# Two of 64 stores issued as two DMAs each in a group-normalisation kernel

## The chip, the cores and the metric

The kernel runs on one core of one Trainium2 chip. The metric is the device time of one execution in microseconds (us), as the median over runs; lower is better.

## The reference

Group normalisation over 128 samples of 1024 channels by 32 x 16 pixels, in 32 groups of 32 channels, all in bfloat16:

```python
def reference(x, g, b):
    G = 32
    B, C, H, W = x.shape[0], x.shape[1], x.shape[2], x.shape[3]
    xr = x.reshape(B, G, C // G, H, W)
    mu = xr.mean(axis=(2, 3, 4), keepdims=True)
    var = ((xr - mu) ** 2).mean(axis=(2, 3, 4), keepdims=True)
    xn = (xr - mu) / jnp.sqrt(var + 1e-5)
    xn = xn.reshape(B, C, H, W)
    return xn * g[None, :, None, None] + b[None, :, None, None]
```

`x` is normal noise times 0.05, `g` is close to 1 and `b` close to 0. Input and output are 134 MB each.

## The kernel before

The work is cut into 64 tiles. A tile `xt` holds two samples: 128 partitions (rows), and in each row 16 channels of 512 pixels, 8192 values or 16 KB. A group of 32 channels lies in two neighbouring rows. A tile is one contiguous piece of 2 MB in the input and in the output, and a row is a contiguous 16 KB of it.

Each tile passes through these steps, one function each:

- `L(i)` loads the tile with one DMA (L121).
- `M1(i)` (L137, ACT) sums the last quarter of each row; `M(i)` (L154, TensorE) sums the rest with an indicator matrix that also adds the two rows of a group. Tiles 0 and 1 are summed by TensorE alone. `R(i)` (L171, DVE) turns the sums into the negative mean.
- `Q(i)` (L189, ACT) squares the centred values and sums them; `Gm(i)` (L206, TensorE) adds the rows of a group; `T(i)` (L221, ACT) takes the square root.
- `A(i)` (L232 to L255, DVE) forms scale and bias for each channel and applies them in place, in 16 instructions, one for each channel of a row.
- `S(i)` stores the tile with one DMA (L267).

The steps of different tiles are interleaved by hand: the main loop's round `s` issues `M1` and `M` of tile `s+1`, `Gm` of `s-1`, `A` of `s-2`, `R` of `s+1`, `Q` of `s`, `T` of `s-1`, then `S` of `s-2` and `L` of `s+7`. A helper, `chain`, ties each instruction to the one before it on the same engine, so every engine runs in the order in which the program is written.

All transfers are issued by one queue, SP's, in that order: nine loads ahead of the loop (and after the first of them four small loads of `g` and `b`), then store, load, store, load. There are eleven `xt` buffers. So `L(i+9)`, which stands behind `S(i)`, goes into the buffer of tile `i-2` and waits until `S(i-2)` has landed, and `S(i+1)` waits in the same queue behind it. After the last load the last nine stores stand in a row, each waiting only for its tile's `A`.

The completion of a transfer is told by a semaphore. There are eight of them, taken in turn, and a transfer that takes one waits, where nothing else ensures it, until the transfer eight places before it has landed. Completion is counted by 16, one for each DMA engine.

The function that the change touches is `S`:

Of the kernel before, what the change touches and what calls it, by code (L numbers as in the profile page):

```python
# [18 lines left out]
PREFETCH = 9  # L19
MM_FREE = 512  # L20
ACT_CHUNKS = 4


@with_exitstack
def kernel(
# [7 lines left out]
    nc = tc.nc  # L33
    P = nc.NUM_PARTITIONS
# [18 lines left out]
    NMM = F // MMN  # L53
    assert 0 <= ACT_CHUNKS < NMM

    x_v = x.rearrange("(t n) (cb k) h w -> t (n cb) (k h w)", n=NS, cb=CB)
    o_v = out.rearrange("(t n) (cb k) h w -> t (n cb) (k h w)", n=NS, cb=CB)
# [19 lines left out]
    def chain(key, inst):  # L77
        prev = last.get(key)
        if prev is not None:
            tc.add_manual_dep(inst.ins, prev.ins.name, nosync, reason="pipeline order")  # L80
        last[key] = inst
        return inst
# [5 lines left out]
        out=ind_f[:].rearrange("p (a c) -> p a c", c=PPG),  # L88
        in_=ones_f[:].rearrange("p (a c) -> p a c", c=PPG),
# [7 lines left out]
        out=ind_f[:].rearrange("p (a c) -> p a c", c=PPG),  # L97
        in_=ind_f[:].rearrange("p (a c) -> p a c", c=PPG),
# [25 lines left out]
    def act_part(i):  # L124
        return ACT_CHUNKS if i >= 2 else 0

# [137 lines left out]

    def S(i):
        st = state[i]
        chain("sp", nc.sync.dma_start(out=o_v[i], in_=st["xt"][:]))  # L267
        state.pop(i - 3, None)

    for i in range(min(PREFETCH, NT)):  # L270
# [16 lines left out]
    for s in range(-1, NT + 2):  # L287
        if 0 <= s + 1 < NT:
            M1(s + 1)
            M(s + 1)  # L290
        if 0 <= s - 1 < NT:
            Gm(s - 1)
        if 0 <= s - 2 < NT:
            A(s - 2)
        if 0 <= s + 1 < NT:
            R(s + 1)
        if 0 <= s < NT:
            Q(s)
        if 0 <= s - 1 < NT:
            T(s - 1)  # L300
        if 0 <= s - 2 < NT:
            S(s - 2)
            if s - 2 + PREFETCH < NT:
                L(s - 2 + PREFETCH)
# [30 lines left out]
```

## Time and profile before

| | |
|---|---|
| median of 3 runs | 639.6 us (639.49 to 640.18) |
| span of the profiled execution, first to last instruction | 637.8 us |
| between that span and the median of the runs | 1.8 us |
| moved by DMA | 268.69 MB, mean 421 GB/s over the span |
| time of ACT's pieces for one tile: L189, L137 | 7.12 and 1.90 us (means) |
| store, median from issue to landing | 28.7 us |
| load, median from issue to landing | 24.2 us |
| issue and landing of the last store | 621.0 us, 15.7 us later |

The profile comes from one execution, its times count from the first instruction. Its page gives the busy time of each engine, the busy share in 40 equal slices of the span, the DMA queues, the chain of work that ended last, and the costliest groups of instructions. The trace behind it also answers for single stretches of time: which instructions ran, what ended the wait before them, and what share of the 16 DMA engines was moving packets. A share of 1.00 means all 16 at work, 0.06 is one of them.

### The profile page before, as it was taken

How to read it: one execution, taken by the hardware profiler on the slowest of the kernel's cores; microseconds unless marked ns; L12 is line 12 of the kernel's file. 1: busy time of each engine (PE TensorE's matmuls, PEld its weight loads, DVE VectorE, ACT ScalarE, POOL GpSimd, SP SyncE). 2: the span in 40 equal slices, each digit the busy share in tenths (PEclk: the TensorE clock that was granted, in tenths of full speed). 3: DMA queues.
4: the chain of work that ended last, by engine and by line, in shares of the span. 5: the costliest groups of instructions: out<-in, count | busy, mean ns of one | idle time of the engine just before them, and what ended most of it. 6: DMA issues, size and time to landing. Idle time of an engine off the chain costs nothing.

```text
span 637.8 us, 3899 instructions
## 1 busy us (share of the span) xinstructions
PE 326.3 (51%) x887; PEld 127.1 (20%) x904; DVE 421.0 (66%) x1349; ACT 590.7 (93%) x318; POOL 1.6 (0%) x6
## 2 busy tenths in 40 slices
PE   4654564556456555645654664464553654635300
PEld 1221122122112212211221222121221221212100
DVE  0086677668667766866776686677667667767680
ACT  1999999999999999999999999999999999999920
POOL 1000000000000000000000000000000000000000
PEclk9767767776776676666667667766766667666655
DMA  8999999999999999999999999999999999999993
GB/s 357 427 427 426 428 425 429 434 428 423 434 429 429 430 431 432 430 431 430 432 429 431 432 431 431 428 431 433 431 429 430 432 432 430 429 432 431 430 423 163
DMA packets 18774, 268.69 MB, mean 421 GB/s; under 512 B 2368, under 2 KB 2368, under 8 KB 2368
## 3 DMA queue, kind: packets, MB, share of 16 engines
q1 hardware_dynamic: 18752, 268.45, 98.7%
q8 instruction: 7, 0.11, 0.1%
q14 instruction: 15, 0.12, 0.0%
HBM read 134.23 MB, written 134.22 MB: 421 GB/s over the span
## 4 chain that ended last, share of the span: by engine, by line
ACT 53%; DMA 23%; issue 17%; DVE 2%; PE 1%; SPq 0%; DVEq 0%; ACTq 0%
ACT ja L189 38%; DMA out_dram<-xt 18%; ACT ja L137 14%; DMA xt<-in_x_dram 5%; DVE xt L255 2%; ACT rstd L221 1%; PE ps L154 1%; SPq L121 0%; DVE jd L171 0%; DVE bia L243 0%; DVE scl L237 0%; DVEq L330 0%; DVE rstd L232 0%; ACTq L137 0%
## 5 line engine op out<-in xcount | busy, mean ns | idle before, releaser
L189 ACT ACTIVATE ja<-xt,negmean 128x8192 bf16<-128x8192 bf16 x64 | 455.8, 7122 | 15.2 <-DVE jd L171 13.2
L154 PE MATMUL ps<-xt,ind_b 128*128 128x512 bf16 x759 | 301.9, 576 | 80.3 <-DMA xt<-in_x_dram 73.1
L255 DVE TENSOR_SCALAR xt<-xt,scl,bia 128x512 bf16<-128x512 bf16 x1024 | 336.6, 408 | 2.6 <-DVE bia L243 0.2
L154 PEld LDWEIGHTS <-ind_b 128*128 128x128 bf16 x776 | 108.6, 146 | 244.8 <-issue 162.4
L232 DVE RECIPROCAL rstd<-rstd 128x1 f32<-128x1 f32 x64 | 10.5, 164 | 169.1 <-ACT rstd L221 169.1
L137 ACT ACTIVATE ja<-xt 128x2048 bf16<-128x2048 bf16 x62 | 117.7, 1898 | 2.6 <-DMA xt<-in_x_dram 2.6
L243 DVE SCALAR_TENSOR_TENSOR bia<-scl,negmean,bet 128x16 f32<-128x16 f32 x64 | 15.0, 235 | 2.3
L237 DVE TENSOR_SCALAR scl<-gam,rstd 128x16 f32<-128x16 f32 x64 | 15.0, 234 | 2.2
L189 ACT ACTIVATION_READ_ACCUMULATOR ja<-xt,negmean 128x1 f32 x64 | 11.9, 186 | 0.0
L137 ACT ACTIVATION_READ_ACCUMULATOR ja<-xt 128x1 f32 x62 | 11.7, 189 | 0.0
L171 DVE TENSOR_SCALAR_CACHE_REDUCE jd<-ps 128x512 bf16<-128x512 f32 x2 | 1.4, 692 | 7.9 <-PE ps L154 7.9
L171 DVE TENSOR_SCALAR_CACHE_REDUCE jd<-ps,ps_170 128x512 bf16<-128x512 f32 x1 | 0.8, 755 | 6.6 <-PE ps_170 L206 6.6
L284 DVE CAST gam<-gam_b 128x16 f32<-128x16 bf16 x1 | 0.2, 174 | 6.4 <-DMA gam_b<-in_g_dram 6.4
L206 PE MATMUL ps_3186<-carry,ind_f 128*128 128x1 f32 x2 | 0.6, 362 | 6.7 <-ACT ja L189 6.7
L206 PE MATMUL ps_2155<-carry,ind_f 128*128 128x2 f32 x2 | 0.6, 362 | 4.8 <-ACT ja L137 4.8
L206 PE MATMUL ps_930<-carry,ind_f 128*128 128x2 f32 x2 | 0.6, 364 | 4.8 <-ACT ja L137 4.8
L206 PE MATMUL ps_1812<-carry,ind_f 128*128 128x2 f32 x2 | 0.6, 364 | 4.7 <-ACT ja L137 4.7
L206 PE MATMUL ps_587<-carry,ind_f 128*128 128x2 f32 x2 | 0.6, 364 | 4.7 <-ACT ja L137 4.7
L206 PE MATMUL ps_1469<-carry,ind_f 128*128 128x2 f32 x2 | 0.6, 362 | 4.6 <-ACT ja L137 4.6
L206 PE MATMUL ps_244<-carry,ind_f 128*128 128x2 f32 x2 | 0.6, 364 | 4.6 <-ACT ja L137 4.6
L206 PE MATMUL ps_1126<-carry,ind_f 128*128 128x2 f32 x2 | 0.6, 364 | 4.6 <-ACT ja L137 4.6
L206 PE MATMUL ps_2008<-carry,ind_f 128*128 128x2 f32 x2 | 0.6, 362 | 4.6 <-ACT ja L137 4.6
(319 smaller groups left out, 126.9 us busy)
## 6 DMA issues: line engine op xcount, KB each, us to landing
xt<-in_x_dram SPq DMA_DIRECT2D x64, 2048.0 KB, 24.2
out_dram<-xt SPq DMA_DIRECT2D x64, 2048.0 KB, 28.7
gam_b<-in_g_dram SPq DMA_DIRECT2D x2, 2.0 KB, 7.1
bet_b<-in_b_dram SPq DMA_DIRECT2D x2, 2.0 KB, 6.7
```

What stands on the lines that cost most here:

```text
L137: nc.scalar.activation(out=ja[:, 0 : na * MMN], in_=xt[:, (NMM - na) * MMN :], func=ACT.Identity, scale=-inv_n, accum_out=carry[:, 1:2],),
L154: nc.tensor.matmul(out=ps[:], lhsT=ind_b[:], rhs=xt[:, k * MMN : (k + 1) * MMN], start=(k == 0), stop=(k == npe - 1),),
L171: nc.vector.tensor_scalar(out=jd[:], in0=st["ps"][:], scalar1=-inv_n, scalar2=seed, op0=ALU.mult, op1=ALU.add, accum_out=negmean[:],),
L189: nc.scalar.activation(out=ja[:], in_=st["xt"][:], func=ACT.Square, bias=st["negmean"][:], scale=1.0, accum_out=carry[:, 0:1],),
L206: nc.tensor.matmul(out=ps2[:, 0:ncol], lhsT=ind_f[:], rhs=st["carry"][:, 0:ncol], start=True, stop=True,),
L221: nc.scalar.activation(out=rstd[:], in_=st["ps2"][:, 0:1], func=ACT.Sqrt, bias=eps_t[:], scale=inv_n),
L232: chain("dve", nc.vector.reciprocal(out=rstd[:], in_=rstd[:]))
L237: nc.vector.tensor_scalar(out=scl[:], in0=gam[:], scalar1=rstd[:], scalar2=None, op0=ALU.mult),
L243: nc.vector.scalar_tensor_tensor(out=bia[:], in0=scl[:], scalar=negmean[:], in1=bet[:], op0=ALU.mult, op1=ALU.add,),
L255: nc.vector.tensor_scalar(out=xt[:, k * HW : (k + 1) * HW], in0=xt[:, k * HW : (k + 1) * HW], scalar1=scl[:, k : k + 1], scalar2=bia[:, k ...
L284: nc.vector.tensor_copy(out=gam[:], in_=gam_b[:])
```

## The change

A table names two tiles and a row for each. The stores of these two tiles are issued as two DMAs, one right behind the other on SP's queue: rows 0 to 119 and 120 to 127 for tile 20, rows 0 to 87 and 88 to 127 for tile 40. The other 62 stores, all loads and all compute are written as before.

```diff
@@ -19,6 +19,7 @@
 PREFETCH = 9
 MM_FREE = 512
 ACT_CHUNKS = 4
+STORE_CUTS = {20: 120, 40: 88}
 
 
 @with_exitstack
@@ -264,7 +265,12 @@
 
     def S(i):
         st = state[i]
-        chain("sp", nc.sync.dma_start(out=o_v[i], in_=st["xt"][:]))
+        cut = STORE_CUTS.get(i)
+        if cut is None:
+            chain("sp", nc.sync.dma_start(out=o_v[i], in_=st["xt"][:]))
+        else:
+            chain("sp", nc.sync.dma_start(out=o_v[i][0:cut], in_=st["xt"][0:cut, :]))
+            chain("sp", nc.sync.dma_start(out=o_v[i][cut:P], in_=st["xt"][cut:P, :]))
         state.pop(i - 3, None)
 
     for i in range(min(PREFETCH, NT)):
```

In the program that results, SP issues 134 DMAs instead of 132, and the two more take a place each in the turn of the eight semaphores. The second pieces and the stores of the next three tiles after each cut carry a wait for the transfer eight places before. The instructions of the other engines are the same, in the same order; only their line numbers move by one and by six.

## The prediction

> **What bounds the kernel now.** I read the page first: its busy table, the DMA rows of the 40 slices and the queue list.
>
> ```profile
> span 637.8 us, 3899 instructions
> PE 326.3 (51%) x887; PEld 127.1 (20%) x904; DVE 421.0 (66%) x1349; ACT 590.7 (93%) x318; POOL 1.6 (0%) x6
> DMA  8999999999999999999999999999999999999993
> DMA packets 18774, 268.69 MB, mean 421 GB/s; under 512 B 2368, under 2 KB 2368, under 8 KB 2368
> q1 hardware_dynamic: 18752, 268.45, 98.7%
> ```
>
> ACT (93%) and the 16 DMA engines (98.7%) are nearly level. To see which ends last, I listed ACT's tile starts (L137) near the end.
>
> ```profile
> 524.21 1.90 ACT L137 ACTIVATE ja<-xt 128x2048 bf16<-128x2048 bf16 x1
> 533.50 1.90 ACT L137 ACTIVATE ja<-xt 128x2048 bf16<-128x2048 bf16 x1
> ...
> 582.72 1.91 ACT L137 ACTIVATE ja<-xt 128x2048 bf16<-128x2048 bf16 x1 [0.32 <-DMA xt<-in_x_dram]
> 592.43 1.91 ACT L137 ACTIVATE ja<-xt 128x2048 bf16<-128x2048 bf16 x1 [0.31 <-DMA xt<-in_x_dram]
> ```
>
> Up to 533.5 us ACT runs at its own pace, 9.29 us a tile; for the last six tiles it waits for loads, at 9.71 us a tile. A tile is one load and one store, 256 rows of 16 KB, 16 rows on each of 16 DMA engines: **9.71 / 16 = 0.607 us for a row on one engine**. Then the windows of the tail, whose last two columns are the DMA engines' mean share and GB/s:
>
> ```profile
> 600.00:620.00 20.00, 1.17 (x4) 1.00 (x4) 16.57 (x55) 9.34 (x7) 0.00 (x0) 0.52 1.01 431
> 626.00:627.00 1.00, 0.00 (x0) 0.00 (x0) 0.00 (x0) 0.00 (x0) 0.00 (x0) 0.50 0.88 377
> 627.00:628.00 1.00, 0.00 (x0) 0.00 (x0) 0.00 (x0) 0.00 (x0) 0.00 (x0) 0.50 0.38 164
> 629.00:630.00 1.00, 0.00 (x0) 0.00 (x0) 0.00 (x0) 0.00 (x0) 0.00 (x0) 0.50 0.15 66
> 633.00:634.00 1.00, 0.00 (x0) 0.00 (x0) 0.00 (x0) 0.00 (x0) 0.00 (x0) 0.50 0.08 33
> 635.00:636.00 1.00, 0.00 (x0) 0.00 (x0) 0.00 (x0) 0.00 (x0) 0.00 (x0) 0.50 0.08 33
> ```
>
> All 16 engines are busy to 620 us, six at 627.5 (0.38 x 16), two at 629.5, and from 631 to 636 only **one**. The list of DMA packets from 630 us confirms it: a row at a time, in even steps.
>
> ```profile
> DMA  0400020020002002000200200020020002000000
> ```
>
> The trace also holds the 16 completions of each transfer, one from each engine. Those of the last store come at 627.1 us for the first, then, the latest five, 628.4, 628.9, 629.7, 631.3 and 636.7. The spread was 0.5 us in the first loads, 5.2 us near 230 us, 8.4 us near 430 us and 10.6 us for the second-last store. So one engine falls behind all the way, and a transfer is complete only when that engine is. The last load, too, was whole only at 592.3, when its fastest engine had been done for 10.1 us. Most of its loss comes in nine steps of about 0.9 us from 158 to 598 us, each 1 to 6 us after one of the queue-14 instruction packets. I call it the straggler. It sets the end: 636.7, 1.1 us before the span closes.
>
> **The change, part by part.**
>
> *The bytes.* Nothing is added or removed: both pieces together hold the same 128 rows. What can move is which engine carries them. A whole transfer gives each engine eight rows. For 120, 8, 88 and 40 rows the trace has no example. I bound it from both sides: dealt as evenly as whole rows allow, no engine gains or loses over about two rows, 1.2 us; dealt in the eight-row shares that every transfer of this trace has, 120 rows fill 15 engines and leave one without, 88 fill 11 and leave five without; the 8 rows make one row each on eight engines, the 40 four each on ten. I take the second, because 120 and 88 are whole multiples of the one share the trace shows, and I take the engines as filled from one end of their order. Against 16 rows for the two stores, the first eight engines then carry 8+1 and 8+4 rows, 21, five more: 5 x 0.607 = **+3.0 us**. The next two carry 20: +2.4 us. One carries 16: 0. Four carry 8: 8 x 0.607 = -4.9 us. The last carries none: **-9.7 us**.
>
> [...]
>
> *The end.* All engines have work queued until the last store, so a shift of rows at tiles 20 and 40 is carried to the end whole. With the straggler the one that carries none, it would finish at 636.7 - 9.7 = 627.0 and another becomes last: 631.3, 629.7 and 628.9 are the next, each +3.0 if it is among the first eight, so 634.3, 632.7 or 631.9. I take the middle one, with the 631.3 engine among those relieved: 636.7 - 632.7 = **4.0 us saved**. The bounds are 2.4 us (634.3) and 5.3 us (628.4 + 3.0).
>
> *Does compute let it?* The last store is issued at 621.0. The shifted engines finish the store before it at 621.3 + 3.7 + 3.0 = 628.0 in the middle case, so they don't wait for the last issue. ACT follows earlier loads: without load waits its last tile could start at 533.50 + 6 x 9.29 = 589.2 rather than 592.4. The loads' latest engine is up to 4 us earlier after the change.
>
> *Two more issues on SP.* Each costs 0.33 to 0.45 us of its queue (the store's issue time, L267). Behind each stands one load, and behind that the next store. They are hidden by the queued work: a load lands a median 24.2 us after its issue, five transfers of 4.86. Price 0; uncovered, 2 x 0.45 = 0.9 us.
>
> *New waits.* The program reuses eight completion semaphores in turn, so the second piece, and the stores of the next three tiles, wait for the transfer eight places earlier, before an unbroken line of loads and stores. For the second piece of tile 20 that is the load of tile 25. The load issued just before had already waited for the store of tile 17, which stands behind tile 25 in every engine's line. The same holds for the others: price 0. The loads that reuse the two buffers wait for both pieces; at most one or four rows on an engine, within the sum.
>
> The sum: 0 + 0 - 4.0. The profiled execution is 637.8 long, 1.8 below the 639.6 median, so 637.8 - 4.0 = 633.8 there and **635.6 us** in the runs.
>
> **Where the straggler sits** no row tells: the trace doesn't number the engines. The same engine is delayed at every step, so the instruction packets come on a fixed one; a fixed duty is more likely given to an end of the order than to its middle, and of the two ends I favour the one that the pieces reach last. That is a choice. [...]
>
> **Rivals.**
> - *The straggler gets more rows* (slower). If it is among the first eight, its end moves to 636.7 + 3.0: 639.6 + 3.0 = 642.6; at place nine or ten 642.0. For it: ten of 16 places. It decides as soon as the straggler's extra exceeds zero, since nothing else ends within 5.4 us. Against it: the argument of the ends.
> - *Two engines read the same part of SBUF.* If in whole transfers each engine always has the same eight rows, engines that are dealt other rows may meet in one part of the memory. If that doubles an eight-row share, each cut store costs 4.9 us more on the loaded engines: 635.6 + 9.7 = 645.3; at half the clash 640.5. For it: the rate of 26.9 GB/s an engine (431 / 16) is nearly steady through the run, as if each had a lane to itself. Against it: by tile 20 the completions are spread over 3.9 us without the straggler, six rows, which thins out a clash. [...]
> - *The pieces are dealt evenly*, so the change moves no work: 639.6 (straggler ±1.2 at most), or the straggler is the place with 16 rows: 639.6. For it: 16 completions of every transfer here; against it: half rows would be needed for 120 and 88.
> - *The straggler loses only eight rows* (among the four): it ends at 631.9, and 632.7 still stands: also 635.6.
>
> **How the numbers follow.** Straggler without rows 0.46, straggler with eight fewer 0.12: together 0.58 for 635.6, with a range of its own from 634.0 (just below 639.6 - 5.3) to 637.2 (639.6 - 2.4). Even or unmoved: 0.10. Straggler with more rows: 0.23. Clash on reads: 0.09. About 0.2% (1.3 us) is what can be told from no change here. So faster 0.58, same 0.10, slower 0.32. The whole range runs from 633.8 to 643.0, over the straggler's 642.6; only a full clash lies outside.
>
> **What would show it.** Right: one engine's late run from 631 to 636 is gone, the DMA share falls from 1 to 0 within a shorter tail, some engines end their last store early, and the last load lands before 592. The short pieces would have fewer completions that follow data. Wrong on dealing: tail unchanged. Wrong on place: the lone engine works 3 us longer. Clash: packets of the two cut stores, near 235 and 425 us, take more than their usual 0.61 us, and the DMA row of those slices falls.

## The result and the profile after

The changed kernel takes 643.87 us (median; 642.93 to 644.09) against 639.55 us of the kernel before on the same chip: 4.3 us more, a ratio of 1.0063 with a 95% interval of 1.005 to 1.0075. It is slower, where the prediction had 635.6 us, and just above its range.

First the rate in 40 slices of 16 us in the kernel before, 423 to 434 GB/s but for the first and the last slice:

```profile
GB/s 357 427 427 426 428 425 429 434 428 423 434 429 429 430 431 432 430 431 430 432 429 431 432 431 431 428 431 433 431 429 430 432 432 430 429 432 431 430 423 163
```

and the span, the rate and the queue of the changed kernel:

```profile
span 642.4 us, 3909 instructions
GB/s 358 429 422 424 429 427 430 431 429 428 432 431 432 428 431 385 431 432 428 434 428 433 431 426 436 429 433 410 392 433 427 432 431 429 433 426 434 429 376 199
q1 hardware_dynamic: 18764, 268.45, 98.6%
```

The bytes are the same. The rate dips at two places, in the 16th slice and in the 28th and 29th, where the cut stores are moved, and in the 39th, before the end. The windows around the two places (the last two columns are the DMA engines' mean share and GB/s), before:

```profile
244.00:256.00 12.00, 5.39 (x14) 2.06 (x14) 7.42 (x25) 11.97 (x9) 0.00 (x0) 0.72 1.00 429
442.00:458.00 16.00, 9.58 (x26) 3.53 (x27) 12.00 (x38) 15.94 (x8) 0.00 (x0) 0.68 1.01 432
```

and after:

```profile
244.00:256.00 12.00, 5.53 (x14) 2.06 (x14) 7.14 (x24) 11.97 (x9) 0.00 (x0) 0.72 0.99 369
442.00:458.00 16.00, 6.07 (x16) 2.24 (x16) 12.31 (x39) 15.94 (x8) 0.00 (x0) 0.68 1.01 379
```

The engines are as busy as before (0.99 and 1.01) and move 12 to 14% less: packets there take longer than their 0.61 us, 0.69 us on average from 242 to 256 us and 0.70 us from 442 to 458 us. No engine stands idle, the rows themselves are slow. Then the windows of the tail, after:

```profile
600.00:620.00 20.00, 3.53 (x13) 2.03 (x11) 15.65 (x52) 14.63 (x7) 0.00 (x0) 0.59 0.94 401
632.00:633.00 1.00, 0.00 (x0) 0.00 (x0) 0.00 (x0) 0.00 (x0) 0.00 (x0) 0.50 0.46 197
634.00:635.00 1.00, 0.00 (x0) 0.00 (x0) 0.00 (x0) 0.00 (x0) 0.00 (x0) 0.50 0.34 147
636.00:637.00 1.00, 0.00 (x0) 0.00 (x0) 0.00 (x0) 0.00 (x0) 0.00 (x0) 0.50 0.27 115
638.00:639.00 1.00, 0.00 (x0) 0.00 (x0) 0.00 (x0) 0.00 (x0) 0.00 (x0) 0.50 0.19 82
640.00:641.00 1.00, 0.00 (x0) 0.00 (x0) 0.00 (x0) 0.00 (x0) 0.00 (x0) 0.50 0.08 33
```

Before, all engines were busy to 620 us. Now the share is already 0.94: engines that are ahead run out of work, since the last stores are issued late, the last one at 626.3 us (621.0 before). And the late ones are later: five engines at 634.5 (0.34 x 16), four at 636.5, three at 638.5, one or two at 640.5. The last completions of the last store, singly, are 637.1, 637.5, 640.1, 641.0 and 641.4 us, where they had been 628.4, 628.9, 629.7, 631.3 and 636.7. The last load is late too: ACT starts its last tile at 597.7 us in place of 592.4.

In this profiled execution the engine that ends last is not the straggler. The straggler can be told by its steps of 0.8 to 1 us behind instruction packets. Those behind the packets at 485.0, 543.6 and 601.6 us appear in the third-latest or second-latest completion, not in the latest. So the straggler ends at 640.98 us, 4.2 us later than its 636.75 before, and another engine ends 0.4 us behind it. That other engine ended at 631.4 us or sooner before the change. Five more rows explain 3.0 of its 10 us; about 7 us have another cause.

The completions also tell how the rows were dealt. With a full transfer 16 data completions come. The 120-row piece has 15, the 8-row piece 8, the 88-row piece 11 and the 40-row piece 10. (Each of these has one completion more, half a microsecond after its issue, before any of its data.)

### The profile page after: what moved, and what is told of

Its sections match the earlier page's. It is cut to its first block, busy times and chain, and to the rows that moved or that the text cites. A ratio compares the mean times of both kernels' runs of the same rounds, so it can differ in the third digit from the quotient of the medians.

```text
span 642.4 us, 3909 instructions
## 1 busy us (share of the span) xinstructions
PE 328.3 (51%) x887; PEld 128.5 (20%) x904; DVE 420.8 (66%) x1349; ACT 591.7 (92%) x318; POOL 1.6 (0%) x6
## 4 chain that ended last, share of the span: by engine, by line
ACT 49%; DMA 27%; issue 15%; DVE 5%; PE 1%; DVEq 0%; SPq 0%; ACTq 0%
ACT ja L190 36%; DMA out_dram<-xt 14%; DMA xt<-in_x_dram 13%; ACT ja L138 13%; DVE xt L256 4%; ACT rstd L222 1%; PE ps L155 1%; DVE jd L172 0%; DVE bia L244 0%; DVE scl L238 0%; DVE rstd L233 0%; DVEq L336 0%; SPq L122 0%; ACTq L138 0%
## 5 line engine op out<-in xcount | busy, mean ns | idle before, releaser
L155 PE MATMUL ps<-xt,ind_b 128*128 128x512 bf16 x759 | 305.1, 581 | 89.5 <-DMA xt<-in_x_dram 86.4
L207 PE MATMUL ps<-carry,ind_f 128*128 128x2 f32 (+1 forms) x128 | 31.7, 318 | 197.0 <-ACT ja L138 185.5
L207 PEld LDWEIGHTS ps<-carry,ind_f 128*128 128x128 f32 x128 | 30.0, 278 | 230.7 <-ACT ja L138 211.2
L172 DVE TENSOR_SCALAR_CACHE_REDUCE jd<-ps,ps 128x512 bf16<-128x512 f32 x62 | 46.3, 746 | 7.1 <-PE ps L207 7.1
L222 ACT ACTIVATE rstd<-ps,eps_t 128x1 f32<-128x1 f32 x64 | 15.4, 241 | 0.5 <-PE ps L207 0.5
L172 DVE DVE_READ_ACCUMULATOR jd<-ps,ps 128x1 f32 x62 | 4.9, 80 | 0.0
```

Of the source, the lines that this page charges most:

```text
L155: nc.tensor.matmul(out=ps[:], lhsT=ind_b[:], rhs=xt[:, k * MMN : (k + 1) * MMN], start=(k == 0), stop=(k == npe - 1),),
L172: nc.vector.tensor_scalar(out=jd[:], in0=st["ps"][:], scalar1=-inv_n, scalar2=seed, op0=ALU.mult, op1=ALU.add, accum_out=negmean[:],),
L207: nc.tensor.matmul(out=ps2[:, 0:ncol], lhsT=ind_f[:], rhs=st["carry"][:, 0:ncol], start=True, stop=True,),
L222: nc.scalar.activation(out=rstd[:], in_=st["ps2"][:, 0:1], func=ACT.Sqrt, bias=eps_t[:], scale=inv_n),
```

## The experiments

Two theories stand against each other. PLACE: the straggler is not among the engines relieved, but among the first eight, which carry five rows more. CLASH: the place does not matter; engines that are dealt other rows than usual slow each other. In all runs the kernel before ran beside the others on the same chip; differences are between medians.

### One cut at a time

The first of the two runs cuts tile 20 alone,

```diff
-STORE_CUTS = {20: 120, 40: 88}
+STORE_CUTS = {20: 120}
```

and the second tile 40 alone:

```diff
-STORE_CUTS = {20: 120, 40: 88}
+STORE_CUTS = {40: 88}
```

> Only tile 20's store is cut, 120 + 8 rows. Theory PLACE (the straggler is one of the first eight engines, so the cut adds rows to the very engine that ends last; nothing else costs): one row more, 0.61 us, 639.55 + 0.6 = 640.2 us. Theory CLASH (the cost is that engines that are dealt other rows than usual disturb each other: in the changed kernel's packets from 242 to 256 us the time above 0.61 us sums to 26 us over 15 engines, 1.7 us each, on average): 641.3 us or more. If both act on the straggler: 641.9.

> Only tile 40's store is cut, 88 + 40 rows. PLACE: the straggler carries 12 rows in place of 8, four more, 2.4 us: 642.0. CLASH alone (from 442 to 458 us the time above 0.61 us sums to 32 us over 11 engines, 2.9 us each): 642.4. Both on the straggler: 644.8. The two cuts are expected to add up to the 4.3 us of the changed kernel.

Measured: 641.24 against 639.78 (ratio 1.0023, 1.0014 to 1.0031), 1.5 us; and 643.02 against 639.78 (1.0046, 1.0034 to 1.0058), 3.2 us. They add up to 4.7 us, which agrees, within the intervals, with the 4.3 of both. Each lies above PLACE, by 0.9 and 0.8 us; the first is clear of noise, while the interval of the second (2.2 to 3.7 us) still holds PLACE's 2.4. So either PLACE and a smaller second cost, or CLASH at about its own price; the next two runs separate these.

### A clash without extra rows, and extra rows without a clash

```diff
-STORE_CUTS = {20: 120, 40: 88}
+STORE_CUTS = {20: 64, 40: 64}
```

> Tiles 20 and 40 are cut in the middle, 64 + 64 rows. If rows are dealt in equal shares to as many engines as divide the count, all 16 engines get four rows of each piece, eight in all, as before, so PLACE expects no change, 639.6. CLASH expects engines to meet in the rows of one half: packets of these two stores well above 0.61 us, the rate of those slices down from 431 GB/s to 340 or less, and 641 to 645 us.

The other run leaves the stores whole and puts eight extra copies between two tensors in device memory behind stores:

```diff
+EXTRA = {12: (8, 1), 16: (8, 1), 20: (8, 1), 24: (8, 1), 28: (8, 1), 32: (8, 1), 36: (8, 1), 40: (8, 1)}
...
+    scr = nc.dram_tensor("scr", (ncopy, rcopy, F + 2048), BF16, kind="Internal").ap()
...
+        rows, times = EXTRA.get(i, (0, 0))
+        for _ in range(times):
+            chain("sp", nc.sync.dma_start(out=scr[nscr[0]][0:rows, 0:F], in_=x_v[i][0:rows]))
+            nscr[0] += 1
```

A pair in the table is the number of rows and of copies.

> No store is cut; eight extra copies of 8 rows of 16 KB from the input to a scratch tensor in device memory, one behind the store of tiles 12, 16, ... 40: one row more on each of the first eight engines each time, and no SBUF in it. PLACE: the straggler carries 8 x 0.607 = 4.9 us more: 644.4 us. If the straggler is one of the other eight engines, as the prediction took it, the end stays where it was unless the second slowest engine (5.4 us ahead) is overtaken: 639.6. CLASH has no part in it.

The halves: 641.65 against 639.78 (1.0034, 1.0019 to 1.005), 1.9 us, 0.9 a cut, with 16 completions for each half and so eight rows a store on every engine. Single runs of this kernel lie further apart than those of the kernel before, from 640.4 to 645.2 us. Its windows at the same two places:

```profile
244.00:256.00 12.00, 5.55 (x14) 2.06 (x14) 7.20 (x24) 11.97 (x9) 0.00 (x0) 0.72 1.00 370
442.00:458.00 16.00, 7.18 (x19) 2.66 (x20) 12.23 (x39) 15.94 (x8) 0.00 (x0) 0.68 1.00 392
```

Nearly the same dip, 370 and 392 GB/s at full share, though not down to the 340 expected. So the dip, which is CLASH's sign, comes without any imbalance.

The extra copies: 644.59 against 639.78 (1.0072, 1.006 to 1.0084), 4.8 us for eight rows, 0.60 a row. PLACE had 4.9, and the prediction's placing of the straggler had 0. The tail of this run:

```profile
632.00:633.00 1.00, 0.00 (x0) 0.00 (x0) 0.00 (x0) 0.00 (x0) 0.00 (x0) 0.50 0.16 66
638.00:639.00 1.00, 0.00 (x0) 0.00 (x0) 0.00 (x0) 0.00 (x0) 0.00 (x0) 0.50 0.08 33
640.00:641.00 1.00, 0.00 (x0) 0.00 (x0) 0.00 (x0) 0.00 (x0) 0.00 (x0) 0.50 0.04 16
```

The lone engine is there as before (a share of 0.06 on average), but works until 641 where it stopped at 636. The straggler took the extra rows: PLACE is shown, and CLASH is a second cost beside it.

### Which engine it is

In the changed kernel the 8-row piece had 8 data completions, one row on each of eight engines. The same extra copies with fewer rows are taken to reach fewer engines in the same way, from the same end. Only the number of rows in the table differs.

> As the run with eight extra copies, but of 7 rows each, so that the eighth engine gets none. If the straggler is one of the first seven: again 4.8 us more, 644.6. If it is the eighth: its end stays, 639.7, unless the second slowest, 5.4 us ahead before, overtakes it with 8 x 0.607 = 4.9 us: at most 640. [...]

> Eight extra copies of 4 rows, so one row more on the first four engines each time. If the straggler is one of these: 639.9 + 4.8 = 644.7. If it is the fifth, sixth or seventh: 640, or a little more if the second slowest overtakes.

> Eight extra copies of 2 rows, one row more on each of the first two engines. If the straggler is one of these: 644.7; if not: 640.

> Eight extra copies of 3 rows, one row more on each of the first three engines. Two rows left the end where it was and four moved it by 4.6 us, so the straggler is the third or the fourth engine: 644.5 if the third, 640 if the fourth.

| rows in each of 8 extra copies | this, us | before, us | ratio (95%) |
|---|---|---|---|
| 8 | 644.59 | 639.78 | 1.0072 (1.006 to 1.0084) |
| 7 | 644.94 | 640.15 | 1.0074 (1.0062 to 1.0086) |
| 4 | 644.48 | 639.85 | 1.007 (1.0056 to 1.0085) |
| 3 | 639.89 | 639.78 | 1.0003 (0.9993 to 1.0012) |
| 2 | 639.88 | 639.85 | 0.9999 (0.999 to 1.0008) |

Three rows cost nothing (639.89 us), four cost the whole 4.6 us (644.48). So the straggler is the fourth engine in the order in which these copies are dealt, number 3 counted from 0. In the trace of the four-row run the latest completion also rises by 0.6 us behind copies, between its larger steps; in that of the three-row run it does not. The runs were made on four chips, two and four rows on one of them and three rows on another, so the place is taken to be the same on each; all five rows of the table agree with that.

The runs with two and three rows carry eight more DMAs than the kernel before, with their issues, semaphores and waits, at no cost (639.88 and 639.89 us), which also clears those parts of the change.

### What the clash is

> Six stores (tiles 8, 16, 24, 32, 40, 48) cut into 64 + 64 rows; every engine keeps eight rows a store. If what is left over beside the extra rows is the clash of engines that are dealt rows other than their own, it grows with the cuts: 0.9 us a cut by the run with two such cuts, 639.9 + 6 x 0.9 = 645.3. If the two-cut run was a stray: 640.

> The same six stores cut by columns, 128 rows of 8 KB each, twice. Each engine keeps its own rows; there are as many DMAs, semaphores and waits as with the cut by rows, and twice the packets. CLASH: no engine meets another, so no change: 639.9, packets of half the size at half the time, and the rate stays at 431 GB/s. If it is the second DMA itself that costs (its issue, its semaphore, its wait), the same 5 us as the cut by rows.

The second of these cuts the same six stores by columns:

```diff
-        chain("sp", nc.sync.dma_start(out=o_v[i], in_=st["xt"][:]))
+        cols = [0, F // 2, F] if i in COLUMN_CUTS else [0, F]
+        for lo, hi in zip(cols, cols[1:]):
+            chain("sp", nc.sync.dma_start(out=o_v[i][:, lo:hi], in_=st["xt"][:, lo:hi]))
```

By rows: 643.36 against 639.85 (1.0057, 1.0035 to 1.0079), 3.5 us, 0.6 a cut; fewer than the 5.4 expected, but clear, with single runs from 640.9 to 647.7 us. By columns: 640.00 (0.9999, 0.9991 to 1.0008), no change. The rates over 100 us show the same, by rows (cuts at tiles 8 to 48)

```profile
100.00:200.00 100.00, 57.25 (x152) 21.37 (x150) 70.13 (x226) 99.67 (x54) 0.00 (x0) 0.68 1.00 419
200.00:300.00 100.00, 57.25 (x154) 21.62 (x154) 72.03 (x230) 99.64 (x53) 0.00 (x0) 0.69 1.01 423
```

and by columns

```profile
100.00:200.00 100.00, 56.64 (x151) 20.95 (x149) 70.06 (x225) 99.67 (x54) 0.00 (x0) 0.68 1.01 430
200.00:300.00 100.00, 57.60 (x154) 21.77 (x154) 71.27 (x228) 99.64 (x53) 0.00 (x0) 0.68 1.01 430
```

Cutting six stores in two DMAs each cost nothing here where all 128 rows stayed in each piece (640.00 against 639.85 us), and 3.5 us where each piece had 64 rows, though the 64-row halves of the two-store run show 16 completions each. That agrees with CLASH, which has engines slow each other when they are dealt other rows. The trace names neither engine nor row, so it is not shown that engines meet in one part of SBUF. Device memory as the place is not excluded either, but the eight-row copies, which go from one tensor there to another, cost no more than their rows (0.60 us each), and the rate stood at 434 and 430 GB/s in the same two windows of that run.

### Relief for the eighth engine

This was run together with the seven-row copies, when the straggler could still have been the eighth engine.

```diff
-STORE_CUTS = {20: 120, 40: 88}
+STORE_CUTS = {20: [96, 117, 124], 40: [96, 117, 124]}
```

> Stores of tiles 20 and 40 in four pieces of 96, 21, 7 and 4 rows: 6 rows on each engine, then 3 and 1 on the first seven, 1 on the first four. The eighth engine carries 6 rows instead of 8, the first seven 10 or 11. If the eighth is the straggler, it ends 4 x 0.607 = 2.4 us earlier, 637.3, plus what the cut itself costs it (0.8 to 0.9 us a cut by the runs with one cut and with two halves): 637.3 to 639.1. If it is among the first seven: 639.8 + 2.4 to 3.6 + 1.7 = 643.9 or more.

The median of six runs, which lie between 648.7 and 658.9 us, is 653.14 against 640.15. The ratio of 1.0169 (1.0141 to 1.0196) makes it 11 us slower. If these pieces are dealt in equal shares from one end, as the completions show equal shares fit for the others (120 rows on 15 engines, 40 on 10), the fourth engine gets 6 + 3 + 1 + 1 = 11 rows a store here, six more in all; at 0.60 us a row that is 3.6 us. This is the author's estimate, and no completions of these pieces are shown. The other 7 us are more than the clash added in the other cuts; the rate was 374 GB/s from 436 to 470 us. How they arise from four pieces was not followed up.

### Why the straggler falls behind

> No store is cut. DVE's 16 instructions a tile that apply scale and bias are 32 of half the width, the same result. Theory FETCH (the straggler falls behind because it also carries the instruction packets of queue 14, about 0.9 us each, and those are DVE's): with 37 DVE instructions a tile in place of 21 some 8 more packets come, and the end moves 5 to 8 us: 645 to 648. Theory RATE (that engine is simply slower at its rows): 639.8, since DVE has room (66% busy) and is not last.

> No store is cut. DVE applies scale and bias in 8 instructions a tile of twice the width, each pair of channels with the first one's scale and bias, so odd channels come out with a neighbour's. FETCH: about 13 DVE instructions a tile in place of 21, some 4 packets fewer, the straggler 3.5 to 4 us earlier: 636. RATE: 639.8.

The loop over the 16 instructions, doubled at half the width,

```diff
-        for k in range(KC):
+        for k in range(2 * KC):
...
-                    out=xt[:, k * HW : (k + 1) * HW],
+                    out=xt[:, k * HW // 2 : (k + 1) * HW // 2],
```

and halved at twice the width:

```diff
-        for k in range(KC):
+        for k in range(0, KC, 2):
...
-                    out=xt[:, k * HW : (k + 1) * HW],
+                    out=xt[:, k * HW : (k + 2) * HW],
```

Doubled: 680.15 us. DVE became the bound, 615.2 us busy of 678.6, and the stores waited 589.0 us for it, so this says nothing of the end. It does show that packets come with DVE's instructions: queue 14 has 24 where it had 15, nine more, and DVE's instructions were the only ones added. The queue's row in the kernel before, then with the instructions doubled, halved, and (further down) with eight of 16 on GpSimd:

```profile
q14 instruction: 15, 0.12, 0.0%
q14 instruction: 24, 0.20, 0.1%
q14 instruction: 12, 0.10, 0.0%
q14 instruction: 18, 0.15, 0.1%
```

Halved: 635.74 against 640.15 (0.9931, 0.9918 to 0.9944), 4.4 us faster, as FETCH had it, with 12 such packets. Since it also changed what DVE computes, the work was then shared with GpSimd, with nothing left out:

```diff
         for k in range(KC):
             chain(
-                "dve",
-                nc.vector.tensor_scalar(
+                "pool" if k >= KC - POOL_CHANNELS else "dve",
+                (nc.gpsimd if k >= KC - POOL_CHANNELS else nc.vector).tensor_scalar(
```

> No store is cut. GpSimd takes the last eight of the 16 instructions a tile that apply scale and bias; DVE keeps eight; same result. FETCH: DVE runs 13 instructions a tile in place of 21, fewer queue-14 packets of its own, and the straggler ends 3 to 4 us earlier, as in the run with half the instructions: 636.5; GpSimd's packets fall on whichever engine carries its fetches. RATE: 639.9. If GpSimd needs more than 9.3 us for eight instructions, it becomes the bound and the run is slower than 645 and says nothing.

> The same with four instructions a tile on GpSimd. FETCH: DVE runs 17 in place of 21, 2 packets fewer, 1.5 to 2 us earlier: 638. RATE: 639.9.

Eight on GpSimd: **637.13** against 639.78 (0.9956, 0.9944 to 0.9969). Four: 638.63 against 639.78 (0.9982, 0.9973 to 0.9991). The end moves with DVE's instruction count, though by 2.7 and 1.2 us rather than 3 to 4 and 1.5 to 2. The tail of the run with eight:

```profile
628.00:629.00 1.00, 0.00 (x0) 0.00 (x0) 0.00 (x0) 0.00 (x0) 0.00 (x0) 0.50 0.23 98
632.00:633.00 1.00, 0.00 (x0) 0.00 (x0) 0.00 (x0) 0.00 (x0) 0.00 (x0) 0.50 0.12 49
634.00:635.00 1.00, 0.00 (x0) 0.00 (x0) 0.00 (x0) 0.00 (x0) 0.00 (x0) 0.50 0.00 0
```

The lone run from 631 to 636 is gone: two engines (0.12 x 16) end almost together, at 633.2 and 633.8. The straggler's steps, most of them of 0.8 to 1 us, can be counted in the latest completions after 150 us. There are nine in the kernel before, 50 to 59 us apart, eight with four instructions moved, 59 to 64 us apart, and five with eight moved, 74 to 84 us apart. With DVE's instructions halved there are five, 83 us apart, and with them doubled the steps come every 30 to 40 us between 180 and 550 us. With eight moved, queue 14 has 18 packets, three more than before and six more than with DVE's instructions halved, where GpSimd had none of the 512 that it has here; so the end follows DVE's instructions and not the number of packets on the queue. RATE, an engine that is simply slow, would have left them as they were.

## Why the prediction was wrong

- **What bounds the kernel** was right: one engine ends alone, and the time follows it, 0.60 us a row as predicted from 9.71 / 16.
- **How the rows are dealt** was right: 15, 8, 11 and 10 engines, filled from one end, +5 rows on the first eight. No trace had shown the one row each on eight engines and the four each on ten before; the completions after the change show the counts. That the engines are filled from one end the completions do not tell, but the extra copies agree with it (three rows 639.89 us, four rows 644.48).
- **Where the straggler sits** is the step that failed. The prediction chose the end of the order, from a general notion of where fixed duties are put, and applied -9.7 us to the straggler. It is the fourth engine, so the term is the +3.0 us of the first eight; the straggler ended 4.2 us later, not 9.7 us earlier. That was the first rival, 642.6 us at 0.23; ten of 16 places spoke for it, and the argument that turned the odds had no row under it.
- **The clash** was held to be an alternative to that rival. It is a companion: beside the 3.0 us of rows, 1.2 us more came on the straggler. The 0.6 to 0.9 us a cut by which the end moved are not the size of the clash. The rate lost in the two windows (60 GB/s over 12 us, 53 over 16) amounts to 1.7 and 2.0 us for an engine on average, and one engine lost about 7 us, more than half of the 9.7 put down for a full clash. Most of it fell on engines that had time to spare before the straggler. So the premise that nothing else ends within 5.4 us did not hold after the cuts: another engine passed the straggler. That it passed by only 0.4 us, so that 3.0 and 1.3 us still add up to the 4.3 measured, is chance. With rivals that can act together, the range should have reached past 642.6 by one clash.
- **That compute lets it** was right for an earlier end only. The last store's issue moved from 621.0 to 626.3 us, behind the late loads; the engines that were ahead waited for it.
- **The issues on SP and the new waits** cost nothing, as predicted: the columns run (640.00 us) and the two- and three-row copies (639.88 and 639.89) carry as many or more.
- **That instruction packets delay the straggler** was seen in the trace beforehand (nine steps of about 0.9 us behind queue-14 packets), but used only to call the straggler fixed. It could have led to asking which instructions they fetch.

## What to carry to other kernels

Here the DMA queue was busy for 98.7% of 16 engines' span, and that mean hid an engine that ended alone, a share of 0.06 from 631 to 636 us. Where DMA is as busy, look at the spread between the first and the last completion of a transfer over time (0.5 us in the first loads here, 10.6 at the second-last store), and at the last microseconds with a share of one in sixteen. Before rows are shifted between engines, look for the late one with a few small extra copies of 2, 4 and 8 rows: that cost a run each here (639.88, 644.48 and 644.59 us) and decided the sign of the term. If a large transfer has to be cut, try it along the columns and keep all 128 rows in each piece, which cost nothing here (640.00 against 639.85 us).

## What was not expected of the hardware

Nine of the 15 instruction packets of queue 14 in the kernel before, 8 KB each and 0.31 us long, are followed within 1 to 6 us by a step of mostly 0.8 to 1.0 us in the latest completion, and the steps are fewer with fewer DVE instructions: eight with four a tile moved to GpSimd, five with eight moved. So these packets seem to be DVE's, to fall on one DMA engine and to delay its data; the trace does not number the engines. From 153 to 598 us the spread between first and last completion grew by these steps from 3.4 to 10.9 us. Why a step is three times as long as its packet stays open. So the number of DVE's instructions helped to set the end of a kernel in which DVE was 66% busy and waited for others: sharing eight of 16 with GpSimd gave 637.13 us, faster than the kernel before and than the changed one.
